# The hi/lo split of the product ab, moved behind two copies of the next f tile, in an attention and two expert blocks kernel

## The chip, the cores and the metric

One core of one Trainium2 chip. The metric is device time of one execution in microseconds (us). Engines: TensorE (PE, its weight loads PEld), VectorE (DVE), ScalarE (ACT), GpSimd (POOL) and SyncE (SP), whose queue issues the DMAs.

## What is computed

The reference runs a packed attention and two expert blocks in fp32, one after the other. Cut to the block that the change touches:

```
x = moe(attention(q, k, v, p))         # 4608 tokens x 512
a = x @ w1                             # 512 x 1024
b = x @ w2
h = (a * b) @ w3                       # 1024 x 1024
out = h @ w_out                        # 1024 x 512
```

## The kernel before

Every fp32 matrix that goes into TensorE is split into a high part (rounded by a copy to fp32r) and a low part (the difference), and each product is three matmuls: high x high, high x low, low x high. The helper `split` (L90) issues the copy on ScalarE (L92) and the subtraction on VectorE or GpSimd (L88).

The second expert block works with w3 @ w_out formed beforehand (`wo3`), so what remains is a, b, their product ab, and ab @ wo3. Tokens are taken in NG2 = 6 groups of 768 (two halves of TH = 384), the 1024 columns of w1 and w2 in NF2 = 8 f tiles of 128. `stage5(g, f)` computes ab of one f tile with a seven-product scheme (Strassen's, in Winograd's form): `PROD` lists the products with their PSUM bank (A, B or C), their weight block and their block of x. Each product is six matmuls of 384 columns (L916). Bank A is written by products 0, 2, 4 and 6, which add up in it; between them ScalarE copies the running sum out (`keep`, L931): s1 after product 0, s2 after product 2, s3 after product 4. Product 2 can overwrite A only when s1 is out, product 4 only when s2 is out, product 6 only when s3 is. Bank B takes products 1 and 3 (copy s5 after product 1), bank C product 5. Three banks are taken per tile out of eight in turn.

The combinations (`comb`, L936) are c12 and c11 on VectorE and c22 on GpSimd; then ab[:, 1] = c12 * c22 on GpSimd (L961) and ab[:, 0] = c11 * A on VectorE (L962), and at the end of the tile ab is split into abh (ScalarE, 128x768) and abl (VectorE). The copies s, the combinations c and ab have one buffer each; abh and abl have eight, one per f tile. When all eight tiles of a group are done, `x2_prep` makes the blocks of x of the next group and `stage7(g)` multiplies ab by wo3 (L978, 144 matmuls of 512 columns) and stores the result. Tile f of ab is first needed by the matmuls of stage7, from the 3f-th on.

In group 0 ScalarE, VectorE and GpSimd also prepare weights: within tile f, `ahead(k)` splits block k of tile f + 1 after product k (`ws_block`: a cast on ScalarE, the subtraction on VectorE for even k, on GpSimd for odd k, and a store), and between tiles `ws_sums` (four adds on VectorE), `split_wo3` and loads run. In the later groups `ahead(k)` only loads the stored blocks (`ws_load`, on SP's queue), 256 KB each, two tiles ahead of their use.

Each engine works its instructions in the order in which the program issues them. In the trace the order on ScalarE between two tiles of group 0 is abh, the cast of wo3, s1, block 0, s5, block 1, s2; in later groups abh, s1, s5, s2. In the views buffer names are shortened: s1, s2, s3, s5 are all `s`, c12, c22, c11 are `c`, banks are `pA`, `pB`, `pC`, and the blocks of x are `xB11`, `xT1`, `xT2`, `xB22`, `xT3`, `xB21`, `xT4` for products 0 to 6, with h and l for the two parts.

Of the kernel before, what the change touches and what calls it, by code (L numbers as in the profile page):

```python
# [38 lines left out]
def packed_attention_moe_kernel(  # L39
# [46 lines left out]
    def sub(out, src, hi, on="dve"):  # L86
        eng = nc.vector if on == "dve" else nc.gpsimd
        eng.tensor_tensor(out=out, in0=src, in1=hi.bitcast(F32), op=ALU.subtract)  # L88

    def split(hi, lo, src, on="act", sub_on="dve"):  # L90
        if on == "act":
            nc.scalar.copy(hi, src)  # L92
        else:
            nc.vector.tensor_copy(hi, src)
        sub(lo, src, hi, sub_on)
# [615 lines left out]
    def load_w12(f):  # L711
        t = vl.tile([128, 2, 2, 256], F32, tag="wf", name=f"w12r{f}")
        nc.sync.dma_start(t.rearrange("p x k n -> p x (k n)"), w12d[f].rearrange("p x c n -> p x (c n)"))
        w12r_t[f] = t

    def ws_sums(f):
        t = w12r_t.pop(f)
        a11, a12, a21, a22 = (t[:, x, kh] for x in range(2) for kh in range(2))
        sa = vl.tile([128, 2, 256], F32, tag="vu", name=f"wsa{f}")
        sb = vl.tile([128, 2, 256], F32, tag="vu", name=f"wsb{f}")  # L720
        tt = nc.vector.tensor_tensor
        tt(out=sa[:, 0], in0=a21, in1=a22, op=ALU.add)
        tt(out=sa[:, 1], in0=sa[:, 0], in1=a11, op=ALU.subtract)
        tt(out=sb[:, 0], in0=a11, in1=a21, op=ALU.subtract)
        tt(out=sb[:, 1], in0=a12, in1=sa[:, 1], op=ALU.subtract)
        wsrc[f] = {"A11": a11, "A12": a12, "A22": a22, "S1": sa[:, 0], "S2": sa[:, 1],
                   "S3": sb[:, 0], "S4": sb[:, 1]}
# [11 lines left out]
    def ws_block(f, k):  # L739

        t = ws_tile(0, f, k)
        split(t[:, 0], t[:, 1], wsrc[f][PROD[k][1]], sub_on="pool" if k % 2 else "dve")
        if f:
            nc.sync.dma_start(wsd[f, k], t.bitcast(F32).rearrange("p h (d n) -> p h d n", d=2))

    def ws_load(g, f, k):
        t = ws_tile(g, f, k)
        nc.sync.dma_start(t.bitcast(F32).rearrange("p h (d n) -> p h d n", d=2), wsd[f, k])
# [18 lines left out]
    def x2_prep(g, part):  # L767
        if part == 0:
            x2_load(g, 0, 0)
            x2_load(g, 0, 1)  # L770
            x2_load(g, 1, 1)
        elif part == 1:
            x2_sub(g, "T1", "B12", "B11")
            x2_split(g, "B11")
            x2_load(g, 1, 0)
            x2_sub(g, "T2", "B22", "T1")
            x2_split(g, "T1")
        elif part == 2:
            x2_sub(g, "T4", "B21", "T2")
            x2_split(g, "T2")  # L780
            x2_split(g, "B22")
        else:
            x2_sub(g, "T3", "B22", "B12")
            x2_split(g, "T3")
            x2_split(g, "B21")
            x2_split(g, "T4")
# [103 lines left out]
    mp = pool("mp", "right")  # L890
    wo3_hi = mp.tile([128, NF2, DM], F32R, name="wo3_hi")
    wo3_lo = mp.tile([128, NF2, DM], F32R, name="wo3_lo")
    ab_t, wo3_t = {}, {}

    def bank(name):
        return psS.tile([128, 512], F32, tag="s", name=name)

    def load_wo3(r):
        t = vl.tile([128, DM], F32, tag="vt", name=f"wo3r{r}")
        nc.sync.dma_start(t, wo3d[1, r])  # L900
        wo3_t[r] = t

    def split_wo3(r):
        split(wo3_hi[:, r], wo3_lo[:, r], wo3_t.pop(r))

    def stage5(g, f):
        bk = {n: bank(f"p{n}{g}_{f}")[:, 0:TH] for n in "ABC"}
        A, Bk, Cb = (bk[n] for n in "ABC")

        def product(k, first):  # L910
            n, _, name = PROD[k]
            xh, xl = x2_t[g, name]
            w = ws_t[f, k]
            for d in range(2):
                for i, (hl, r) in enumerate(((0, xh), (0, xl), (1, xh))):
                    nc.tensor.matmul(bk[n], lhsT=w[:, hl, 128 * d:128 * d + 128], rhs=r[:, d],  # L916
                                     start=(first and d == 0 and i == 0), stop=(d == 1 and i == 2),
                                     skip_group_check=not first)

        def ahead(k):  # L920

            if g == 0 and f + 1 < NF2:
                ws_block(f + 1, k)
            n = (NF2 - 1) * g + f + 1
            ng, nf = divmod(n, NF2 - 1)
            if f and 0 < ng < NG2:
                ws_load(ng, nf + 1, k)

        def keep(name, t):
            o = mp.tile([128, TH], F32, tag=name, name=f"{name}_{g}_{f}")  # L930
            nc.scalar.copy(o, t)  # L931
            return o

        def comb(name, t, o, op=ALU.add, on=nc.vector):
            r = mp.tile([128, TH], F32, tag=name, name=f"{name}_{g}_{f}")
            on.tensor_tensor(out=r, in0=o, in1=t, op=op)  # L936
            return r

        product(0, True)
        s1 = keep("s1", A)  # L940
        ahead(0)
        product(1, True)
        s5 = keep("s5", Bk)
        ahead(1)
        product(2, False)
        s2 = keep("s2", A)
        ahead(2)
        product(3, False)
        c12 = comb("c12", Bk, s2)
        ahead(3)  # L950
        product(4, False)
        s3 = keep("s3", A)
        c22 = comb("c22", s5, s3, on=nc.gpsimd)
        ahead(4)
        product(5, True)
        c11 = comb("c11", Cb, s1)
        ahead(5)
        product(6, False)
        ahead(6)
        ab = mp.tile([128, 2, TH], F32, tag="ab", name=f"ab{g}_{f}")  # L960
        nc.gpsimd.tensor_tensor(out=ab[:, 1], in0=c12, in1=c22, op=ALU.mult)  # L961
        nc.vector.tensor_tensor(out=ab[:, 0], in0=c11, in1=A, op=ALU.mult)  # L962
        abh = mp.tile([128, 2, TH], F32R, tag="abh", name=f"abh{g}_{f}", bufs=NF2)
        abl = mp.tile([128, 2, TH], F32R, tag="abl", name=f"abl{g}_{f}", bufs=NF2)
        split(abh, abl, ab)
        ab_t[f] = (abh, abl)

    def stage7(g):
        for tb in range(2 * TH // 128):
            j, cols = tb // 3, slice(128 * (tb % 3), 128 * (tb % 3) + 128)  # L970
            t = bank(f"po{g}_{tb}")
            for f in range(NF2):
                abh, abl = ab_t[f]
                for a, w, first, last in (
                    (abh, wo3_hi, f == 0, False), (abh, wo3_lo, False, False),
                    (abl, wo3_hi, False, f == NF2 - 1),
                ):
                    nc.tensor.matmul(t, lhsT=a[:, j, cols], rhs=w[:, f], start=first, stop=last)  # L978
            o = vl.tile([128, DM], F32, tag="vu", name=f"o{g}_{tb}")
            nc.scalar.copy(o, t)  # L980
            r0 = 2 * TH * g + 128 * tb
            nc.sync.dma_start(out[r0:r0 + 128, :], o)

    load_wo3(0)
    with tc.manual_schedule(engines=M0):
        for g in range(NG2):
            for f in range(NF2):
                stage5(g, f)
                if g == 0:
                    if f + 2 < NF2:  # L990
                        ws_sums(f + 2)
                    if f + 3 < NF2:
                        load_w12(f + 3)
                    split_wo3(f)
                    if f + 1 < NF2:
                        load_wo3(f + 1)
            if g + 1 < NG2:
                for part in range(4):
                    x2_prep(g + 1, part)
            stage7(g)  # L1000
# [39 lines left out]
```

## Time and profile before

| | us |
|---|---|
| median of 3 runs | 1483.64 (1482.56 to 1486.55) |
| profiled execution | 1484.05 |
| its span | 1482.3 |
| PE busy in the span | 1403.5 (95%) |
| DVE, ACT, POOL busy | 817.5, 667.4, 483.9 |
| TensorE clock granted, mean | 0.975 |

Starts are counted from the start of the span. A timeline row reads: start, duration, engine, line, operation, written <- read, form; in brackets the idle time of that engine before it and who ended it. Matmuls overlap, so a row's duration is longer than the step from one to the next. PE is the row of the matmuls, PEld that of the weight loads, and a wait can stand at either.

### The profile page before, as it was taken

Reading aid. Unit: us, or ns where it says so; the run is one execution under the profiler, and the core shown is the slowest. Engines: PE = TensorE matmul, PEld = TensorE weight load, DVE = VectorE, ACT = ScalarE, POOL = GpSimd, SP = SyncE. Lnnn points to the kernel's source line nnn. Section 1 sums busy time; section 2 is a strip of 40 time slices with the busy share of each in tenths; the row PEclk is TensorE's granted clock in tenths of the full one; section 3 lists DMA queues with packets and bytes.
Section 4 is the critical chain, followed back from the end, with each engine's and each line's share of the span. In section 5 each row is a group of like instructions: output and inputs, shape, how many; then the busy total and the mean of one; then the engine's idle time right before and its main releaser. Section 6 shows DMA issues by size and latency. Waiting matters only on the chain.

```text
span 1482.3 us, 25352 instructions
## 1 busy us (share of the span) xinstructions
PE 1403.5 (95%) x9872; PEld 1305.7 (88%) x9872; DVE 817.5 (55%) x1220; ACT 667.4 (45%) x1113; POOL 483.9 (33%) x353
## 2 busy tenths in 40 slices
PE   6767989999999999999999999899999999999998
PEld 4446979998999999999989998889989999899997
DVE  2548899968876446656366647852333413334230
ACT  4556564536745346554464434533323323333231
POOL 0325443445543345445343223521202112021120
PEclk8778999999999999999999999999999999999999
DMA  9996565667543332125252425873836538366451
GB/s 246 216 231 187 154 176 168 188 198 204 147 131 81 113 74 74 51 65 171 87 162 94 128 79 178 287 253 122 246 109 205 186 125 246 105 206 186 126 165 43
DMA packets 193624, 230.26 MB, mean 155 GB/s; under 512 B 88288, under 2 KB 121056, under 8 KB 193504
## 3 DMA queue, kind: packets, MB, share of 16 engines
q1 hardware_dynamic: 193504, 228.64, 52.3%
q8 instruction: 78, 1.28, 0.4%
q14 instruction: 42, 0.34, 0.1%
HBM read 179.04 MB, written 49.55 MB: 154 GB/s over the span
## 4 chain that ended last, share of the span: by engine, by line
PE 74%; DVE 5%; DMA 3%; ACT 2%; issue 2%; POOL 0%; SPq 0%; ACTq 0%; DVEq 0%
PE px L632 16%; PE pA L916 14%; PE po L978 13%; PE pB L916 7%; PE pg L607 7%; PE pv L607 7%; PE pC L916 3%; PE pc L382 3%; DMA raw_w<-in_moe_w_dram 1%; DMA w12d<-w12t 1%; DVE cl L88 1%; DVE u L614 1%; PE psq L171 1%; DVE vx_w L305 1%; DVE acc L642 1%
## 5 line engine op out<-in xcount | busy, mean ns | idle before, releaser
L88 POOL TENSOR_TENSOR ul<-u,uh 128x576 fp32r<-128x576 f32 x96 | 146.2, 1527 | 216.3 <-ACT uh L92 215.8
L936 POOL TENSOR_TENSOR c<-s,s 128x384 f32<-128x384 f32 x48 | 48.7, 1014 | 388.6 <-ACT s L931 387.8
L632 PE MATMUL px<-uh,woh 128*128 128x288 f32 x768 | 165.9, 298 | 4.7 <-DVE cl L88 2.1
L632 PE MATMUL px<-ul,woh 128*128 128x288 f32 x768 | 165.3, 297 | 1.3 <-POOL ul L88 1.3
L632 PE MATMUL px<-uh,wol 128*128 128x288 f32 x768 | 164.8, 296 | 0.0
L88 POOL TENSOR_TENSOR wl<-wf,wh 128x1024 fp32r<-128x1024 f32 x48 | 118.5, 2468 | 122.0 <-ACT wh L92 92.3
L88 DVE TENSOR_TENSOR cl<-pc,ch 64x1024 fp32r<-64x1024 f32 x144 | 120.5, 864 | 56.1 <-ACT ch L395 52.4
L632 PEld LDWEIGHTS px<-uh,woh 128*128 128x128 f32 x768 | 123.8, 189 | 7.5 <-DVE cl L88 2.6
L632 PEld LDWEIGHTS px<-ul,woh 128*128 128x128 f32 x768 | 124.1, 190 | 1.5 <-POOL ul L88 1.5
L632 PEld LDWEIGHTS px<-uh,wol 128*128 128x128 f32 x768 | 124.3, 190 | 0.0
L931 ACT COPY s<-pA 128x384 f32<-128x384 f32 x144 | 68.7, 477 | 118.0 <-PE pA L916 118.0
L936 DVE TENSOR_TENSOR c<-s,pB 128x384 f32<-128x384 f32 x48 | 26.5, 552 | 156.6 <-PE pB L916 156.6
L978 PE MATMUL po<-wo_hi,abl 128*128 128x512 f32 x288 | 112.3, 390 | 0.0
L978 PE MATMUL po<-wo_lo,abh 128*128 128x512 f32 x288 | 112.2, 390 | 0.0
L978 PE MATMUL po<-wo_hi,abh 128*128 128x512 f32 x288 | 112.1, 389 | 0.0
L642 DVE TENSOR_TENSOR acc<-acc,px 128x576 f32<-128x576 f32 x96 | 71.0, 746 | 64.5 <-PE px L632 64.3
L92 ACT CAST uh<-u 128x576 fp32r<-128x576 f32 x96 | 64.6, 673 | 84.0 <-DVE u L614 83.6
L614 DVE TENSOR_TENSOR u<-u,pv 128x576 f32<-128x576 f32 x96 | 72.1, 752 | 45.4 <-PE pv L607 41.0
L88 POOL TENSOR_TENSOR wol<-wof,woh 128x512 fp32r<-128x512 f32 x48 | 64.9, 1363 | 82.2 <-ACT woh L92 70.8
L607 PE MATMUL pv<-aTh,ch 128*128 128x288 f32 x384 | 84.1, 301 | 7.3 <-ACT u L612 5.8
L92 ACT CAST abh<-ab 128x768 fp32r<-128x768 f32 x48 | 40.1, 835 | 109.8 <-POOL ab L961 109.8
L607 PE MATMUL pg<-aTh,ch 128*128 128x288 f32 x384 | 85.2, 304 | 2.1 <-DVE u L614 1.2
(345 smaller groups left out, 3668.6 us busy)
## 6 DMA issues: line engine op xcount, KB each, us to landing
ws<-wsd SPq DMA_DIRECT2D x245, 256.0 KB, 3.1
wf<-Wd SPq DMA_DIRECT2D x36, 512.0 KB, 3.4
raw_w<-in_moe_w_dram SPq DMA_DIRECT2D x32, 512.0 KB, 4.6
wsd<-ws SPq DMA_DIRECT2D x49, 256.0 KB, 2.7
raw_wo<-in_moe_w_out_dram SPq DMA_DIRECT2D x20, 512.0 KB, 4.3
km<-in_k_dram SPq DMA_DIRECT2D x16, 576.0 KB, 9.7
vm<-in_v_dram SPq DMA_DIRECT2D x16, 576.0 KB, 9.9
qr<-in_q_dram SPq DMA_DIRECT2D x128, 72.0 KB, 3.5
```

Source lines behind the costliest of these rows:

```text
L88: eng.tensor_tensor(out=out, in0=src, in1=hi.bitcast(F32), op=ALU.subtract)
L92: nc.scalar.copy(hi, src)
L171: nc.tensor.matmul(t[32 * at:32 * at + 32, hf, 0:HS], lhsT=PT[:, 32 * hq:32 * hq + 32], rhs=qT[:, hq // 2, HS * hf:HS * hf + HS], start=Tr ...
L382: nc.tensor.matmul(t[:, kt], lhsT=a[:, kt, P, :], rhs=w[:, kt], start=(x == 0), stop=(x == 2))
L607: nc.tensor.matmul(t[:, hf, 0:HS], lhsT=w[:, b % 2, Q, cols], rhs=x[:, Q, hf, :], start=first, stop=last,)
L614: nc.vector.tensor_tensor(out=u, in0=u, in1=t[:, :, 0:HS], op=ALU.mult)
L632: nc.tensor.matmul(t[:, hf, 0:HS], lhsT=w[:, 128 * d:128 * d + 128], rhs=x[:, hf, :], start=first, stop=last,)
L642: nc.vector.tensor_tensor(out=o, in0=o, in1=t[:, :, 0:HS], op=ALU.add)
L916: nc.tensor.matmul(bk[n], lhsT=w[:, hl, 128 * d:128 * d + 128], rhs=r[:, d], start=(first and d == 0 and i == 0), stop=(d == 1 and i == 2) ...
L931: nc.scalar.copy(o, t)
L936: on.tensor_tensor(out=r, in0=o, in1=t, op=op)
L978: nc.tensor.matmul(t, lhsT=a[:, j, cols], rhs=w[:, f], start=first, stop=last)
```

## The change

The split of ab is no longer issued at the end of its tile. stage5 appends it to a list, and the next tile issues it behind its copies s1 and s5 (and, in group 0, behind the cast of weight block 0). After the last tile of a group it is issued before x2_prep, as before. In group 0 it now comes after the sums, the split of wo3 and the loads that stand between tiles. No instruction is added or taken away.

```
-    ab_t, wo3_t = {}, {}
+    ab_t, wo3_t, ab_split = {}, {}, []
...
         product(1, True)
         s5 = keep("s5", Bk)
+        while ab_split:
+            ab_split.pop()()
         ahead(1)
...
-        split(abh, abl, ab)
         ab_t[f] = (abh, abl)
+        ab_split.append(lambda: split(abh, abl, ab))
...
                     if f + 1 < NF2:
                         load_wo3(f + 1)
+            ab_split.pop()()
             if g + 1 < NG2:
                 for part in range(4):
                     x2_prep(g + 1, part)
```

## Rows read from the trace of the kernel before

**Rows 1.** Page: span, and the chain that ended last, by line.
```profile
span 1482.3 us, 25352 instructions
...
PE px L632 16%; PE pA L916 14%; PE po L978 13%; PE pB L916 7%; PE pg L607 7%; PE pv L607 7%; PE pC L916 3%; PE pc L382 3%; DMA raw_w<-in_moe_w_dram 1%; DMA w12d<-w12t 1%; DVE cl L88 1%; DVE u L614 1%; PE psq L171 1%; DVE vx_w L305 1%; DVE acc L642 1%
```

**Rows 2.** Busy by stretch: PE, PEld, DVE, ACT, POOL, then clock, DMA, GB/s.
```profile
912.30:983.00 70.70, 60.61 (x340) 58.19 (x339) 52.51 (x90) 38.41 (x95) 34.68 (x37) 1.00 0.79 279
...
1015.70:1482.30 466.60, 462.57 (x2400) 424.27 (x2399) 144.19 (x204) 146.20 (x259) 80.97 (x80) 1.00 0.52 162
```

**Rows 3.** Waits in the first group: who waited for whom, us, times, longest.
```profile
ACT abh L92 <- POOL ab L961: 16.4, 7, 2.6
...
PE pA L916 <- ACT s L931: 10.1, 7, 1.7
```

**Rows 4.** Waits of PEld in the later groups.
```profile
PEld pA L916 <- ACT s L931: 9.7, 38, 0.3
```

**Rows 5.** Timeline of the first two tiles of group 2.
```profile
1108.08 0.34 PE L916 MATMUL pA<-xB11h,ws 128*128 128x384 f32 x1
...
1109.99 0.19 PEld L916 LDWEIGHTS pA<-xT2h,ws 128*128 128x128 f32 x1
...
1110.37 0.48 ACT L931 COPY s<-pB 128x384 f32<-128x384 f32 x1 [0.56 <-PE pB L916]
...
1112.08 0.19 PEld L916 LDWEIGHTS pA<-xT3h,ws 128*128 128x128 f32 x1
...
1115.21 1.00 POOL L961 TENSOR_TENSOR ab<-c,c 128x384 f32<-128x384 f32 x1
...
1115.37 0.34 PE L916 MATMUL pA<-xB11h,ws 128*128 128x384 f32 x1
...
1116.24 0.84 ACT L92 CAST abh<-ab 128x768 fp32r<-128x768 f32 x1 [2.28 <-POOL ab L961]
...
1116.98 0.47 ACT L931 COPY s<-pA 128x384 f32<-128x384 f32 x1
...
1117.51 0.19 PEld L916 LDWEIGHTS pA<-xT2h,ws 128*128 128x128 f32 x1 [0.22 <-ACT s L931]
```

**Rows 6.** Timeline, PEld, group 1: the load for product 2, two tiles.
```profile
1032.46 0.19 PEld L916 LDWEIGHTS pA<-xT2h,ws 128*128 128x128 f32 x1 [0.27 <-ACT s L931]
...
1039.96 0.19 PEld L916 LDWEIGHTS pA<-xT2h,ws 128*128 128x128 f32 x1 [0.27 <-ACT s L931]
```

**Rows 7.** Timeline, PE, group 0: first matmul of tiles 0, 1 and of stage7.
```profile
912.48 0.34 PE L916 MATMUL pA<-xB11h,ws 128*128 128x384 f32 x1
...
919.90 0.34 PE L916 MATMUL pA<-xB11h,ws 128*128 128x384 f32 x1
...
982.85 0.39 PE L978 MATMUL po<-wo_hi,abh 128*128 128x512 f32 x1
```

**Rows 8.** Timeline, ACT, group 0, from one tile to the next.
```profile
930.63 0.83 ACT L92 CAST abh<-ab 128x768 fp32r<-128x768 f32 x1 [2.31 <-POOL ab L961]
...
931.89 0.47 ACT L931 COPY s<-pA 128x384 f32<-128x384 f32 x1
...
932.26 0.41 ACT L92 CAST ws<-w12r 128x256 fp32r<-128x256 f32 x1
...
932.57 0.48 ACT L931 COPY s<-pB 128x384 f32<-128x384 f32 x1
```

**Rows 9.** Timeline, DVE, group 0: abl of two tiles.
```profile
931.50 0.96 DVE L88 TENSOR_TENSOR abl<-ab,abh 128x768 fp32r<-128x768 f32 x1 [1.30 <-ACT abh L92]
...
940.47 0.96 DVE L88 TENSOR_TENSOR abl<-ab,abh 128x768 fp32r<-128x768 f32 x1 [1.30 <-ACT abh L92]
```

**Rows 10.** Timeline, group 0: weight subtractions on POOL and DVE.
```profile
934.99 1.01 POOL L88 TENSOR_TENSOR ws<-wsb,ws 128x256 fp32r<-128x256 f32 x1 [0.80 <-ACT ws L92]
...
934.99 0.41 DVE L88 TENSOR_TENSOR ws<-w12r,ws 128x256 fp32r<-128x256 f32 x1
...
935.33 0.95 DVE L88 TENSOR_TENSOR ws<-wsa,ws 128x256 fp32r<-128x256 f32 x1
```

More of the change, by code (lines that the diff above doesn't have):

```diff
@@ L892, in packed_attention_moe_kernel @@
     wo3_lo = mp.tile([128, NF2, DM], F32R, name="wo3_lo")
-    ab_t, wo3_t = {}, {}
+    ab_t, wo3_t, ab_split = {}, {}, []
     def bank(name):
@@ L943, in stage5 @@
         s5 = keep("s5", Bk)
+        while ab_split:
+            ab_split.pop()()
         ahead(1)
@@ L964, in stage5 @@
         abl = mp.tile([128, 2, TH], F32R, tag="abl", name=f"abl{g}_{f}", bufs=NF2)
-        split(abh, abl, ab)
         ab_t[f] = (abh, abl)
+        ab_split.append(lambda: split(abh, abl, ab))
     def stage7(g):
@@ L996, in packed_attention_moe_kernel @@
                         load_wo3(f + 1)
+            ab_split.pop()()
             if g + 1 < NG2:
```

## The prediction

> **What bounds the kernel now.** I read the chain of work that ended last first: it is TensorE's nearly all the way, and the lines of the second block (L916 with banks A, B and C, L978) are 37% of the span [rows 1]. So only time in which TensorE stands still is for sale. The table by stretches says where that is: the first group (912.3 to 983.0) has PE busy 60.6 of 70.7 us, all the later groups together 462.6 of 466.6 us, with a granted clock of 1.00 in both, that is the 2.4 GHz level [rows 2]. The waits name the reason. In the first group the matmuls of product 2 (xT2) wait seven times for a ScalarE copy out of bank A, 10.1 us, and in the same stretch the cast abh waits seven times for POOL's half of ab, 16.4 us [rows 3]. In the later groups no matmul row has a wait, but TensorE's weight loads do: 38 times, 9.7 us, again for that copy [rows 4].
>
> The timeline of one later tile shows how the two waits hang together. All times of a tile are counted from its first matmul, T. In the first tile of a group nothing is late: 1108.08 to 1115.37, 7.29 us for 42 matmuls; the load for product 2 starts at T+1.91, s5 is copied at T+2.29, the load for product 4 starts at T+4.00 [rows 5]. In the second tile ScalarE first stands at the cast abh of the tile before: POOL's ab begins at 1115.21, lasts 1.00, the cast starts at 1116.24 and s1 only at 1116.98, T+1.61. It ends at 1117.45, the load that overwrites bank A starts 0.06 later at 1117.51, which is T+2.14 instead of T+1.91 [rows 5]. Tiles further on have a wait of 0.27 and a period of 7.50 (1032.46 to 1039.96) [rows 6]: 0.21 over 7.29, so the first 0.06 of a late load costs nothing and the rest is lost whole.
>
> The first group has the same chain, longer: 912.48 to 982.85 is 70.37 us [rows 7] against 8 x 7.29 = 58.3, so 12.1 us lost. There the cast starts late behind POOL (930.63, after 2.31 us of waiting), then stands the cast of wo3, and s1 starts at 931.89 [rows 8].
>
> **The change part by part.** Nothing is added: 48 casts and 48 subtractions stay, no DMA is moved (the split issues none), and what SP's queue holds keeps its order. What moves is the place in two queues: on ScalarE the cast abh goes from before s1 to behind s5 of the next tile, on VectorE the subtraction abl goes from behind ab to just ahead of the work for block k = 1, 2 and so before c12. POOL's queue is the same.
>
> Removed: the wait for POOL ahead of s1. s1 can then start when product 0 is done. In the undisturbed tile the same ScalarE copy of the next bank started at T+2.29, one product (1.04 us) later, so s1 starts at T+1.25 and ends at T+1.73; with 0.06 that is before T+1.91. The product 2 stall goes everywhere.
>
> Added: a cast between s5 and s2, and s2 gates product 4, which writes bank A again. Later groups: s5 starts at T+2.29; ScalarE starts the next instruction 0.37 after a copy (931.89 to 932.26 [rows 8]), so the cast starts at T+2.66; the next one starts 0.74 after a cast (1116.24 to 1116.98 [rows 5]), so s2 starts at T+3.40, ends at T+3.88, and the load may start at T+3.94. It is due at T+4.00. Nothing is lost, with a margin of 0.06 and the free 0.06. This handover, copy to cast without a gap, is in no row: the bound from below is this 0; from above, if ScalarE ran them end to end without overlap (0.48 + 0.84 + 0.48 from T+2.29, 4.09, and 0.06), the load is 0.15 late and 0.09 is lost per tile, 35 x 0.09 = 3.2 us. I take 0, since the copy, cast and copy rows of the first group all start before the one ahead has ended [rows 8].
> POOL's ab has ended by T+0.84 (1115.21 + 1.00 against 1115.37), long before T+2.66, so the cast finds its input and no wait comes with it.
>
> First group: one more instruction stands between cast and s2, the cast for block k = 1, 0.31 (932.26 to 932.57 [rows 8]). s2 then starts at T+3.71, ends at 4.19, the load starts at 4.25, 0.25 late, and 0.19 to 0.20 is lost. This holds for six tiles (the last has no blocks left): 1.2 us. The first tile, which has no split in front of it (912.48 to 919.90, 7.42 [rows 7]), keeps its 0.1. So of 12.1 us 10.8 come back. The cast of wo3 slips into the idle time before s1, where it now stands without the POOL wait.
>
> Later groups: 9.7 us of late loads less 38 x 0.06 is 7.4; three of the 38 waits are beyond one a tile (35 tiles) and belong to something else, 0.2: 7.2 us.
>
> VectorE's queue in the first group is what is next late. Its subtraction abl starts at 931.50 and 940.47, a period of 8.97, each after 1.30 of waiting for the cast [rows 9]: 7.67 us of queue a tile, against a new tile of 7.29 + 0.20 = 7.49. VectorE so falls behind by 0.18 a tile. It matters when c11 of a tile (which reads the single s1 buffer) ends after the next s1 wants to start, at T+1.25. Down the queue c11 ends about when the next tile starts, and 6 x 0.18 = 1.1 us later in the last: inside 1.25. I take no loss.
> But 7.67 is made of instructions lengthened by POOL: a 256-column subtraction takes 0.41 alone and 0.95 beside POOL's, and ends 0.28 after POOL's has ended (936.00); POOL's ran 1.01 [rows 10]. The abl and the sums change their neighbours on POOL. The Trainium skill, "SBUF — State Buffer", section "Who interferes with whom", says that a VectorE instruction with two SBUF inputs and a GpSimd one that reads SBUF exclude each other, the second blocking until the first has finished; these rows agree. By it the tile could become the length of the two queues in turn, which is the first rival.
>
> **Sum.** 10.8 + 7.2 = 18.0 us. The profiled execution took 1484.05 us, 1.7 more than its span; 1484.05 - 18.0 = 1466.05. The median of the three runs is 0.4 below the profiled one: 1465.6.
>
> **The rivals.** *VectorE and POOL bound the first group.* For it: a queue of 7.67 against 7.49, both in each other's way [rows 9, 10]. Each us of queue beyond 7.49 comes through after the 1.25 of slack is used. At 8.3 a tile: 6 x 0.8 - 1.25 = 3.6 us, 1469.2. At 8.97, the length of a tile now and the upper bound, since the same work fits into it with idle time left: 6 x 1.48 - 1.25 = 7.6, 1473.2. Against it: POOL stands idle for much of the group (34.7 busy of 70.7 [rows 2]) and the moved abl lands where POOL has only one block's subtraction to do.
>
> *The stall goes on at product 4 in the later groups.* The handover is as slow as its upper bound or somewhat slower (an added wait on two engines): 0.09 to 0.20 a tile, 3 to 7 us back, 1469 to 1473. The first group keeps its gain.
>
> *Slower: the cast before s2 costs more than the wait before s1 did.* Place: every tile but the first of a group, at the load for product 4. Let x be what a later tile then loses; the first group's six tiles lose x more than 0.2. Break even is 35 (0.21 - x) + 10.8 - 6x = 0, x = 0.44, that is a cast and its handover 0.56 longer than 0.84. If the cast took twice its time there, x = 0.72 and 41 x 0.72 - 18 = 11.5 us slower, 1495. For it: nothing but that no row shows a cast in that place. Against it: the casts run 0.83 to 0.84 in both kinds of group [rows 5, 8], and their input is there.
>
> *The change does not do what it says:* the queues are ordered otherwise than the program has them, and the cast stays before s1: 1483.6. Against it: cast, s1, block cast, s5 stand in the trace in the program's order [rows 8].
>
> **How the numbers follow.** Forecast (1463.5 to 1468) 0.72; VectorE and POOL 0.12; product 4 in the later groups 0.10; slower 0.03; nothing changed 0.03. The forecast's lower end is all 12.1 and 7.7 back, 1484.05 - 19.8 - 0.4, a little rounded down. The range runs from there over the first two rivals to their upper ends, 1463.5 to 1473; outside are about 0.1. A measurement of this kernel tells 0.3% (4.5 us) from no change: all of the forecast and of the first two rivals is beyond that, so faster 0.93, within 0.3% 0.04 (nothing changed, and a little of the rivals), slower 0.03.
>
> **What would show it.** Right: s1 at T+1.25 in every tile and no wait of product 2; later tiles of 7.29 and groups of 58.3 between first matmul and first output matmul; the first group at about 59.6 with loads for product 4 0.25 late in six tiles; the cast following s5 within 0.4. Wrong: waits of product 4 in the later groups (the handover), c11 ending after T+1.25 and s1 waiting for VectorE in the first group (the queues in turn), a cast waiting for POOL in its new place, or a granted clock under 1.00 in the second block.

## The result, and the profile after

The changed kernel takes 1465.63 us (median of six, 1460.42 to 1470.25) against 1486.05 (six, 1482.56 to 1487.44): a ratio of 0.9864, 95% interval 0.9836 to 0.9893. Run again beside another kernel it took 1465.39 (five) against 1483.76 (nine), 0.9872 (0.9853 to 0.9891).

Whole times of this kernel spread by up to 10 us, and in the profiles the spread arises ahead of the change: the first matmul of the second block came between 906.4 and 916.5 us in the profiles of all the kernels here, which have the same code before it. (The other executions have no profile.) So I measure from that matmul to the last one of the block, and inside it from the first matmul of a group to its first output matmul (eight tiles):

| us | block | group 0 | groups 1 to 5 | stage7 of group 0 |
|---|---|---|---|---|
| before | 565.4 | 70.37 | 59.75 to 59.88 | 32.69 |
| after | 547.6 | 59.83 | 58.24 to 58.38 | 32.99 |
| after, run again | 548.2 | 59.97 | 58.24 to 58.39 | 33.41 |

The block is 17.8 us shorter (the forecast was 18.0). The span of the profiled execution fell by 13.8 only, because its second block began at 916.46 and that of the kernel before at 912.48 [rows 7].

Behind the change the line numbers of the changed kernel are 2 higher than those of the kernel before (L961 is L963, L962 L964, L978 L980).

The span on the page of the changed kernel:

```profile
span 1468.5 us, 25358 instructions
```

The table by stretches of the changed kernel, first group and later groups (columns as in [rows 2]):

```profile
916.30:976.30 60.00, 60.00 (x340) 58.04 (x339) 52.72 (x90) 38.46 (x95) 38.01 (x37) 1.00 0.90 319
...
1009.00:1464.50 455.50, 455.47 (x2402) 426.24 (x2401) 141.11 (x204) 142.30 (x258) 81.14 (x80) 1.00 0.52 165
```

PE was busy 60.6 of 70.7 us in the first group and 462.6 of 466.6 in the later ones [rows 2]; it is now busy in the whole of both. VectorE's 52.7 us are the same work in 60.0 us of time; from the second to the seventh tile its gaps add up to 0.03 to 0.04 us a tile (1.33 in the kernel before), and nearly all its idle time is in the first and the last tile.

Waits of the changed kernel (engine, line, waited for: us, times, longest) in the first group with its stage7:

```profile
ACT wo_hi L92 <- DMA wo3r<-wo3d: 9.1, 5, 4.4
...
PEld pA L916 <- ACT s L931: 1.6, 6, 0.3
...
PEld po L980 <- DVE abl L88: 0.4, 1, 0.4
```

PEld's waits of the changed kernel in the later groups:

```profile
PEld pA L916 <- ACT s L931: 0.5, 3, 0.2
```

The 10.1 us before matmuls and 16.4 us before the cast in the first group [rows 3] are gone. The six loads that still wait there are of two kinds: in the second to the fifth tile it is the load for product 4, 0.28 each; in the sixth and the seventh it is still the load for product 2, 0.21 and 0.29, now behind the cast of wo3 (below). Of the 9.7 us and 38 waits of the later groups [rows 4] three waits, 0.5 us, are left. Two rows are new: the cast of wo3 waits for its load, and a load of stage7 waits for abl.

The timeline of a later tile of the changed kernel, with T = 1107.62 (to compare with [rows 5]):

```profile
1107.46 1.01 POOL L963 TENSOR_TENSOR ab<-c,c 128x384 f32<-128x384 f32 x1
1107.62 0.34 PE L916 MATMUL pA<-xB11h,ws 128*128 128x384 f32 x1
...
1108.90 0.48 ACT L931 COPY s<-pA 128x384 f32<-128x384 f32 x1 [2.68 <-PE pA L916]
...
1109.95 0.48 ACT L931 COPY s<-pB 128x384 f32<-128x384 f32 x1 [0.57 <-PE pB L916]
...
1110.33 0.84 ACT L92 CAST abh<-ab 128x768 fp32r<-128x768 f32 x1
...
1111.07 0.48 ACT L931 COPY s<-pA 128x384 f32<-128x384 f32 x1
...
1111.20 0.96 DVE L88 TENSOR_TENSOR abl<-ab,abh 128x768 fp32r<-128x768 f32 x1 [2.83 <-ACT abh L92]
...
1111.61 0.19 PEld L916 LDWEIGHTS pA<-xT3h,ws 128*128 128x128 f32 x1
...
1114.90 0.34 PE L916 MATMUL pA<-xB11h,ws 128*128 128x384 f32 x1
```

s1 starts at T+1.28 where it stood at T+1.61. The cast follows s5 by 0.38, s2 follows the cast by 0.74, with no wait printed at either. s2 starts at T+3.45, ends 1111.55, and the load for product 4 starts 0.06 later at T+3.99, unprinted as a wait and just in time. The period is 7.28.

The timeline of the changed kernel in the first group on ScalarE, from the tile with T = 931.40 into the next, T = 938.91 (to compare with [rows 8]):

```profile
932.68 0.48 ACT L931 COPY s<-pA 128x384 f32<-128x384 f32 x1 [1.19 <-PE pA L916]
...
933.74 0.48 ACT L931 COPY s<-pB 128x384 f32<-128x384 f32 x1 [0.27 <-PE pB L916]
934.11 0.84 ACT L92 CAST abh<-ab 128x768 fp32r<-128x768 f32 x1
934.85 0.41 ACT L92 CAST ws<-wsa 128x256 fp32r<-128x256 f32 x1
935.15 0.48 ACT L931 COPY s<-pA 128x384 f32<-128x384 f32 x1
...
939.62 0.62 ACT L92 CAST wo_hi<-wo3r 128x512 fp32r<-128x512 f32 x1 [1.13 <-DMA wo3r<-wo3d]
940.20 0.48 ACT L931 COPY s<-pA 128x384 f32<-128x384 f32 x1
```

The load for product 4 in the first of these tiles, on PEld:

```profile
935.69 0.19 PEld L916 LDWEIGHTS pA<-xT3h,ws 128*128 128x128 f32 x1 [0.28 <-ACT s L931]
```

ScalarE and the load for product 2 in the sixth tile, T = 953.94:

```profile
955.02 0.62 ACT L92 CAST wo_hi<-wo3r 128x512 fp32r<-128x512 f32 x1 [1.51 <-DMA wo3r<-wo3d]
955.55 0.47 ACT L931 COPY s<-pA 128x384 f32<-128x384 f32 x1
...
956.08 0.19 PEld L916 LDWEIGHTS pA<-xT2h,ws 128*128 128x128 f32 x1 [0.21 <-ACT s L931]
```

VectorE from the tile with T = 931.40 into the next (to compare with [rows 9]):

```profile
931.42 0.54 DVE L936 TENSOR_TENSOR c<-s,pC 128x384 f32<-128x384 f32 x1
...
935.53 1.49 DVE L88 TENSOR_TENSOR abl<-ab,abh 128x768 fp32r<-128x768 f32 x1
936.93 0.96 DVE L88 TENSOR_TENSOR ws<-wsa,ws 128x256 fp32r<-128x256 f32 x1
```

POOL beside abl:

```profile
935.33 0.86 POOL L88 TENSOR_TENSOR ws<-wsa,ws 128x256 fp32r<-128x256 f32 x1 [2.07 <-ACT ws L92]
```

s2 starts at T+3.75 with the cast for block 1 ahead of it. In the sixth tile the cast of wo3 has waited 1.51 for its load, s1 behind it starts at T+1.61 instead of T+1.28, and product 2 is late; the seventh tile has the same (1.59 of waiting, s1 at T+1.69). These two tiles take 7.52 and 7.55, little more than the 7.51 of those that lose their time at product 4. On VectorE c11 of the tile before ends at 931.96, T+0.56; abl takes 1.49 instead of 0.96 [rows 9].

### The profile page after: what moved, and what is told of

It reads as the page before. It is cut to its first block, busy times and chain, and to the rows that moved or that the text cites. A ratio compares the mean times of both kernels' runs of the same rounds, so it can differ in the third digit from the quotient of the medians.

```text
span 1468.5 us, 25358 instructions
## 1 busy us (share of the span) xinstructions
PE 1394.9 (95%) x9872; PEld 1307.0 (89%) x9872; DVE 812.5 (55%) x1220; ACT 664.7 (45%) x1113; POOL 487.7 (33%) x353
## 3 DMA queue, kind: packets, MB, share of 16 engines
q8 instruction: 78, 1.28, 0.4%
## 4 chain that ended last, share of the span: by engine, by line
PE 74%; DVE 5%; DMA 3%; issue 2%; ACT 1%; POOL 0%; SPq 0%; DVEq 0%; ACTq 0%
PE px L632 16%; PE pA L916 14%; PE po L980 13%; PE pB L916 7%; PE pg L607 7%; PE pv L607 7%; PE pC L916 3%; PE pc L382 3%; DMA raw_w<-in_moe_w_dram 2%; DVE cl L88 1%; PE psq L171 1%; DVE u L614 1%; DVE vx_w L305 1%; DVE acc L642 1%; DVE vx_w L312 0%
## 5 line engine op out<-in xcount | busy, mean ns | idle before, releaser
L980 PE MATMUL po<-wo_hi,abl 128*128 128x512 f32 x288 | 112.3, 390 | 0.0
L980 PE MATMUL po<-wo_lo,abh 128*128 128x512 f32 x288 | 112.2, 389 | 0.0
L980 PE MATMUL po<-wo_hi,abh 128*128 128x512 f32 x288 | 112.1, 389 | 0.0
L88 DVE TENSOR_TENSOR abl<-ab,abh 128x768 fp32r<-128x768 f32 x48 | 49.2, 1025 | 105.4 <-ACT abh L92 105.3
L612 ACT ACTIVATE u<-pg 128x576 f32<-128x576 f32 x96 | 62.6, 652 | 54.9 <-PE pg L607 52.0
```

Of the source, the lines that this page charges most:

```text
L612: nc.scalar.activation(u, t[:, :, 0:HS], AF.Silu)
```

## The experiments

The figures of each run are read from one profiled execution, inside the second block.

**One part alone: group 0.** The split is deferred in group 0 and left at the end of its tile elsewhere.

```
         ab_split.append(lambda: split(abh, abl, ab))
+        if g > 0:
+            ab_split.pop()()
...
-            ab_split.pop()()
+            while ab_split:
+                ab_split.pop()()
```

> The split is deferred in group 0 alone; in the later groups it stands at the end of its tile, as before. If the gain is the sum of two separate stalls, group 0 takes 59.8 us between its first matmul and the first output matmul (as in the changed kernel), each later group 59.8 (as in the kernel before): 10.5 us of the gain. If the gain needed the whole queue moved, or came from the start of the block, group 0 would not keep its 59.8.

Group 0 took 60.05 (0.2 over the 59.8 expected, all of it in one tile of 7.78, explained further down), the later groups 59.75 to 59.89, the block 555.1: 10.3 us of the gain.

**The other part alone: the later groups.** The condition is g == 0.

> The split is deferred in the later groups alone. If the two stalls are separate: group 0 at 70.4 us, each later group at 58.3, 7.3 us of the gain. If the later groups had gained only because group 0 ended sooner, they would stay at 59.8.

Group 0 took 70.36, the later groups 58.24 to 58.39, the block 557.9: 7.5 us. 10.3 and 7.5 make the 17.8 of the whole change; the two stalls are separate.

**A longer way between s5 and s2.** One more copy behind the cast, in the 35 later tiles that have one.

```
         while ab_split:
             ab_split.pop()()
+        if g > 0 and f > 0:
+            nc.scalar.copy(mp.tile([128, TH], F32, tag="pad", name=f"pad{g}_{f}"), s1)
```

> One more ScalarE copy of 384 columns stands behind the cast in each of the 35 tiles of the later groups that have one. In the changed kernel s2 starts at T+3.45 and the load for product 4 starts at T+3.99, with no wait. If s2 gates product 4 and that load is just in time, 0.37 for a copy less the 0.06 that a late load costs nothing, 0.31 a tile: later groups at 60.4, 10.9 us slower than the changed kernel. If ScalarE had room there, as its 44% of busy time suggests, the groups stay at 58.3.

PEld's waits of this kernel in the later groups:

```profile
PEld pA L916 <- ACT s L931: 13.6, 36, 0.4
```

The later groups took 60.62 to 60.63, every one of the 35 tiles 7.62, 0.34 over 7.28, 11.5 us in the five groups (expected 10.9). So s2 does gate product 4, and of a delay of 0.37 only 0.03 was free, where the forecast had 0.12; a part of that was used up by s5, which starts at T+2.33 and not at T+2.29. The 0.34 is more than the 0.21 to 0.22 that such a tile lost in the kernel before: one copy too many in this place, and the later groups are slower than they were. Group 0, which this edit does not touch, took 60.83 instead of 59.83; why is told with the runs of the earlier load.

**Behind s1 alone.** The split is issued ahead of s5 and of the cast for block 0.

```
         s1 = keep("s1", A)
+        while ab_split:
+            ab_split.pop()()
...
         s5 = keep("s5", Bk)
-        while ab_split:
-            ab_split.pop()()
```

> The split is issued behind s1, ahead of s5 and of the cast for block 0. Later groups: the cast from T+1.62, s5 from T+2.36 instead of T+2.29, s2 at T+3.33: 58.3 us, as in the changed kernel. Group 0: POOL's half of ab ends at T+1.86 there (933.26 against 931.40 in the changed kernel), so the cast would wait for it, s5 would start at about T+2.95 and end at T+3.43, while product 3 overwrites bank B from T+2.95: 0.4 to 0.5 us a tile lost there, 61.5 to 62.5 us. If it is only s2 and product 4 that limit a tile, group 0 stays at or under 59.8.

PEld's waits of this kernel in group 0 and its stage7, for bank B:

```profile
PEld pB L916 <- ACT s L931: 3.3, 7, 0.5
```

The timeline of this kernel in the fourth tile, T = 936.40 (s1 starts at 937.69):

```profile
937.07 1.20 POOL L963 TENSOR_TENSOR ab<-c,c 128x384 f32<-128x384 f32 x1
...
938.29 0.84 ACT L92 CAST abh<-ab 128x768 fp32r<-128x768 f32 x1
...
939.34 0.47 ACT L931 COPY s<-pB 128x384 f32<-128x384 f32 x1
...
939.86 0.19 PEld L916 LDWEIGHTS pB<-xB22h,ws 128*128 128x128 f32 x1 [0.49 <-ACT s L931]
```

The later groups took 58.24 to 58.39, group 0 61.39: loads of bank B wait seven times, up to 0.5 us each (3.3 in all), for the late s5. In the later groups one copy ahead of the cast is enough. In group 0 the cast starts as POOL's ab ends, 0.60 after s1 instead of 0.37 to 0.38. That is 0.23 of the 0.60 by which s5 is late (T+2.94 instead of T+2.34); the rest is that the cast abh and the cast for block 0 both stand ahead of s5. So POOL's lateness is less than half of the reason there, and the second copy earns 1.5 us. Stage7 of group 0 took 34.24 in this run, 1.3 more than in the changed kernel, with the cast of wo3 waiting up to 5.6 us for its load.

**Behind s2.** The same two lines stand after s2.

> The split is issued behind s2 instead of s5. If the 0.2 us that six tiles of group 0 still lose is the cast standing ahead of s2 (s2 at T+3.75 instead of T+3.33), it goes: group 0 at 58.6 to 58.8 us, the later groups stay at 58.3, since s3 is due only at T+5.41. If VectorE and GpSimd bound group 0, nothing changes there (59.8), or it grows, since abl then stands ahead of block 2 and c12 as before.

Group 0 took 59.43, the later groups 58.24 to 58.37, stage7 of group 0 34.09 instead of 32.99, the block 548.2: nothing gained. No load for product 4 waited any more, yet the tiles took 7.42 and not 7.28. In this run the matmuls of the first six tiles stepped by 0.174 and 0.179 us in turn, 0.1767 in the mean (7.42 over 42), instead of the 0.173 to 0.174 of other runs, without a wait and at a granted clock of 1.00; what slowed them is open. The last tile already shows the next bound, in the timeline of this kernel:

```profile
962.83 0.48 ACT L931 COPY s<-pA 128x384 f32<-128x384 f32 x1 [1.35 <-DVE c L936]
...
972.80 0.62 ACT L92 CAST wo_hi<-wo3r 128x512 fp32r<-128x512 f32 x1 [5.48 <-DMA wo3r<-wo3d]
...
974.21 0.19 PEld L980 LDWEIGHTS po<-wo_hi,abh 128*128 128x128 f32 x1 [1.00 <-ACT abh L92]
```

ScalarE stands idle 1.35 us until c11 is out, and s1 starts at T+1.48 (T = 961.35) instead of T+1.28. Stage7 waits for the cast, which stands, as in the changed kernel, behind a cast of wo3 that waited for its load: 5.48 here, 4.37 there.

**The same with an earlier load of wo3.**

```
         ahead(1)
+        if g == 0 and f + 1 < NF2:
+            load_wo3(f + 1)
...
-                    if f + 1 < NF2:
-                        load_wo3(f + 1)
```

> As the kernel with the split behind s2, and the load of the next block of wo3 is issued after block 1 of the tile instead of at its end. If stage7 of group 0 lost 1.4 us there because the cast of wo3 waited 5.5 us for its load with the split queued behind it, stage7 of group 0 returns from 34.1 to 32.7 us. If the matmuls of group 0 step slower (0.1767 instead of 0.1735 us) because TensorE no longer pauses there, group 0 stays at 59.4; if that was chance, it comes to 58.4.

Stage7 came back to 32.69. Group 0 did not come to 58.4: its second to fourth tile took 7.28 (so the slow step does not come with the order alone; it shows in this run only from 951.5 to 958.4), then 7.33, 8.20, 7.93 and 8.01 followed, 60.73 in all.

The timeline of this kernel on ScalarE shows s1 of the fifth and the seventh tile (T = 941.10 and 956.63), at T+1.48 and T+2.08:

```profile
942.58 0.48 ACT L931 COPY s<-pA 128x384 f32<-128x384 f32 x1 [1.39 <-DVE c L936]
...
958.71 0.48 ACT L931 COPY s<-pA 128x384 f32<-128x384 f32 x1 [2.03 <-DVE c L936]
```

Its waits in group 0 give the one who ended them:

```profile
ACT s L931 <- DVE c L936: 5.5, 3, 2.0
...
PEld pA L916 <- ACT s L931: 2.3, 3, 0.9
```

On VectorE, abl of the fourth and of the fifth tile of this kernel:

```profile
939.02 0.95 DVE L88 TENSOR_TENSOR abl<-ab,abh 128x768 fp32r<-128x768 f32 x1
...
946.59 1.49 DVE L88 TENSOR_TENSOR abl<-ab,abh 128x768 fp32r<-128x768 f32 x1
```

s1, due 1.28 us into a tile, waits for VectorE's c11. With the pause of 0.2 us at product 4 gone, VectorE can't follow: its gaps are 0.03 to 0.04 us a tile, and from one c11 to the next it takes 7.56, more than 7.28, and then 8.02 to 8.11, once abl has slipped beside a subtraction on POOL. The tile takes VectorE's time: the first rival, one step behind the change.

**What VectorE's queue costs.** The subtraction abl is done twice in group 0.

```
-        ab_split.append(lambda: split(abh, abl, ab))
+        ab_split.append(lambda: (split(abh, abl, ab), sub(abl, ab, abh) if g == 0 else None))
```

> The subtraction abl is done twice in group 0, 0.88 us more for VectorE a tile. If VectorE's queue is nearly full there but off the path (c11 ends at T+0.56 to T+0.86 of the next tile, s1 wants to start at T+1.25), the slack of 0.4 to 0.7 is used up in the first tile and the rest comes through: 6 x 0.88 less 0.6, 4 to 5 us, group 0 at 64 to 65, with s1 waiting for c11. If VectorE still had idle time as in the kernel before (1.30 a tile), group 0 would stay under 60.5. The later groups stay at 58.3.

The timeline of this kernel, one s1 on ScalarE:

```profile
944.84 0.48 ACT L931 COPY s<-pA 128x384 f32<-128x384 f32 x1 [2.78 <-DVE c L936]
```

VectorE around and after it, c11 first and the doubled abl last:

```profile
944.19 0.54 DVE L936 TENSOR_TENSOR c<-s,pC 128x384 f32<-128x384 f32 x1
...
947.25 1.23 DVE L88 TENSOR_TENSOR wo_lo<-wo3r,wo_hi 128x512 fp32r<-128x512 f32 x1
948.40 0.96 DVE L88 TENSOR_TENSOR ws<-w12r,ws 128x256 fp32r<-128x256 f32 x1
949.28 2.63 DVE L88 TENSOR_TENSOR abl<-ab,abh 128x768 fp32r<-128x768 f32 x2
```

POOL beside it:

```profile
947.17 0.76 POOL L88 TENSOR_TENSOR ws<-wsa,ws 128x256 fp32r<-128x256 f32 x1 [2.05 <-ACT ws L92]
948.16 0.92 POOL L88 TENSOR_TENSOR ws<-wsb,ws 128x256 fp32r<-128x256 f32 x1 [0.23 <-ACT ws L92]
949.55 1.55 POOL L936 TENSOR_TENSOR c<-s,s 128x384 f32<-128x384 f32 x1 [0.47 <-ACT s L931]
```

Group 0 took 69.56, not 64 to 65. The slack was gone in the third tile (7.95), as expected, but from there on a tile took 9.33, not 7.51 + 0.88: longer than a tile of the kernel before. ScalarE stands idle 2.78 until c11, which ended at 944.73, and s1 starts at T+3.41 (T = 941.43) instead of T+1.28; VectorE's gaps are 0.07 us a tile. Later s copies mean later casts and later subtractions on POOL, which, as the rows show side by side, now fall on wo_lo (1.23 instead of 0.68) and on block 0 (0.96 instead of 0.41); the c22 that starts with abl takes 1.55 instead of 1.02 to 1.16. Other instructions of VectorE get shorter (the first sum 0.41 instead of 0.77), but by less: 0.88 us of work cost 1.8 us of time. Stage7 of group 0 took 34.53, since it also waits for the later abl.

**The changed kernel again, and with the earlier load of wo3 alone.**

> The changed kernel with the same earlier load of wo3 alone. Stage7 of group 0 returns from 33.0 to 32.7 us, and the cast of wo3 in group 0 no longer waits for its load (9.1 us in the changed kernel, hidden but for 0.4). Group 0 stays at 59.8, since those waits ended before s1 was due.

> The changed kernel once more, in the same rounds as the next. From the first matmul of the second block to the last one 547.6 us (565.4 in the kernel before), so 17.8 us less than before; what the whole time shows beside that comes from the first 900 us, whose length differed by up to 10 us between the profiles of kernels that are alike there. Ratio to the kernel before 0.988, between 0.985 and 0.991. If the change also shortened something ahead of the second block, the difference is over 20 us again.

> The changed kernel with the load of the next block of wo3 behind block 1 of the tile. 547.3 us in the second block, 0.3 us less than the changed kernel, all of it in stage7 of group 0; in whole times not to be told from it: ratio to the kernel before 0.988, between 0.985 and 0.991.

The first and the third of these kernels are the same, the changed kernel with the earlier load; the second is the changed kernel repeated.

In the repetition one tile of group 0 took 7.72 instead of 7.51; its timeline on ScalarE:

```profile
943.42 0.62 ACT L92 CAST wo_hi<-wo3r 128x512 fp32r<-128x512 f32 x1 [1.76 <-DMA wo3r<-wo3d]
943.95 0.47 ACT L931 COPY s<-pA 128x384 f32<-128x384 f32 x1
```

The cast of wo3 waits for its load, and s1 behind it is late, at T+1.86 (T = 942.09); product 2 waits 0.45. The run with group 0 alone has the same in a tile of 7.78 (1.83 of waiting), the run with the added copy in two, of 8.04 and 8.03 (2.07 and 2.08), and the changed kernel in its sixth and seventh tile (1.51 and 1.59). So the premise of the first expectation, that those waits ended before s1 was due, was wrong; its figures came out. With the load behind block 1, group 0 took 59.78 and 59.80, without such a tile and with all six waits of 0.28 at product 4, and stage7 32.69; the block took 547.3 both times, 0.3 under the changed kernel and 0.9 under its repetition. In whole times that can't be told: 1464.21 us, ratio 0.9872 (0.9854 to 0.9890), against 1465.39 and 0.9872 (0.9853 to 0.9891) for the changed kernel.

## Why the prediction was right

**The bound and what was for sale.** Right. The gain lies in the two stalls read from the waits, 10.3 and 7.5 us by the experiments with one part alone, forecast 10.8 and 7.2.

**Removed: s1's wait.** Right in the later groups and in most of group 0: s1 at T+1.28, forecast T+1.25, and no wait at product 2. Not right everywhere: in one or two tiles of group 0 in each run of the changed order with the late load of wo3, s1 still comes late and product 2 waits, 0.21 and 0.29 in the changed kernel, no longer for POOL but behind the cast of wo3 (see the missing term).

**Added: the cast ahead of s2, later groups.** The result is right (no loss), the margin was not. Copy to cast took 0.38 and cast to copy 0.74, as read from other pairs; but s5 starts 0.04 later in a tile that follows another, so the load starts on the dot. The added copy shows what was at stake: 0.34 a tile, 11.5 us.

**Group 0.** Where the load for product 4 is what waits, it waits 0.28, forecast 0.25, and the tile takes 7.51, forecast 7.49; with the earlier load of wo3 that is so in all six tiles, in the changed kernel in four. The sum for the group was 59.6, measured 59.83.

**The three odd waits.** Right: what is beyond one wait a tile was set aside, and the same three tiles (the last of group 1, the fifth of group 4, the last of group 5) still take 0.13 more, each with one load that waits 0.18 for s2 or s3. Their sum in the forecast was 7.2, the later groups alone gave 7.5.

**VectorE next late.** The conclusion held, the working did not. I had c11 end with the tile and slip by 0.18 a tile into a slack of 1.25. Measured, it ends at T+0.56 in the third tile, at T+0.86 in the last, so nearly half of the slack was used from the start; the kernel before had that already, as its timeline shows (c11 ends at 938.28, T+0.56):

```profile
937.72 0.34 PE L916 MATMUL pA<-xB11h,ws 128*128 128x384 f32 x1
937.74 0.54 DVE L936 TENSOR_TENSOR c<-s,pC 128x384 f32<-128x384 f32 x1
```

And it slips by about 0.05 only, as VectorE's queue takes 7.55 and not 7.67. The abl became longer beside POOL (1.49), which the forecast feared, other instructions shorter.

**A term that was missing.** The cast of wo3 was to slip into idle time before s1. It does, but it now comes ahead of its load's landing, 9.1 us of waiting, five times; in the sixth and the seventh tile it held s1 back, in the last abh stands behind it, and stage7 waits 0.43 for abl. In the repetition it held s1 in one tile, but longer. I had looked at the instructions on ScalarE's queue and not at what each needs. Price against the kernel with the earlier load: 0.3 us in the one run of the changed kernel and 0.9 in the other; group 0 and its stage7 together lost 0.3 in the run with group 0 alone and 1.0 in the run with the added copy, which have the same group 0.

**The rivals.** VectorE and POOL did not bound the changed kernel, but they would at the next 0.2 us: the tile then takes 7.9 to 8.2, shown in one run. My price for it, each us beyond 7.49 passed on, was too low: 0.88 us passed on 1.8. Product 4 in the later groups did not stall. The slower case put its break-even at 0.44 lost a tile; the added copy, with 0.34, lies on the near side of it: its block took 559.8, still less than 565.4.

**The total.** 1465.6 forecast, 1465.6 measured; with a spread of whole times of 10 us so close a hit is luck. The kernel before moved too: 1483.64 was its median ahead of the forecast, 1486.05 beside the changed kernel, so whole times fell by 20.4 there and by 18.4 in the repetition. The block is the fair comparison: 18.0 forecast, 17.8 and 17.2 measured. The lower end of the range puts the later groups at 7.7, a figure that the forecast does not work out; 7.5 was measured.

## What to carry to other kernels

An in-order engine that makes a copy which frees an accumulator should have nothing ahead of that copy that waits for a slower engine or for a load; put such work behind the copies whose successors are due latest, and add up the handovers to the next due time, since the margin can be hundredths of a microsecond. When the first stall is gone, look at what each instruction that moved forward needs (a load), and at the queue that was resting during the stall: here VectorE went from 1.3 us of rest a tile to nearly none. A queue that collides with another engine's gets longer not only by the work that is added to it, but by new collisions too.

## What was not expected of the hardware

A subtraction of two SBUF operands on VectorE beside POOL's took 1.49 us instead of 0.96 and 1.23 instead of 0.68, and POOL's c22 1.55 instead of 1.02 to 1.16. The Trainium skill, "SBUF — State Buffer", section "Who interferes with whom", says that such pairs exclude each other; these lengths agree roughly (the abl of 1.49 ends at 937.02, 0.83 after the subtraction on POOL that had begun before it, and takes 0.96 alone). No run here shows what the loss is once a whole loop of copies, casts and subtractions shifts with it, other than the 1.8 us for 0.88.

In one run the matmuls of 384 columns stepped by 0.174 and 0.179 us in turn over 45 us of the first group, with nothing waiting and a granted clock of 1.00, and by 0.173 to 0.174 again after the next pause, a step of 0.28 at 955.5. A run with the same order of the split stepped so for 7 us only, from one pause of the matmuls to another. The cause is open.
